# Projections with omega: the two heads of a pair alternate on the array's two halves, all of k before all of q

## The chip, the cores and the metric

The kernel runs on one core of one Trainium2 chip, with float32 throughout. A core has a matrix engine (TensorE, "PE" in the profile, with its weight loads as "PEld"), a vector engine (DVE), a scalar engine (ACT), a general engine (POOL) and a queue engine (SP), each with an instruction stream of its own; they wait for one another by semaphores. Matrix products land in PSUM, from which DVE and ACT fetch them. The metric is the device time of one execution in microseconds; lower is better.

## What is computed

Two blocks follow each other. The first is attention by random features for 8 batches of 8 heads, 576 rows, 64 columns; the second mixes its output by a Fourier transform over rows and columns, normalises it and sends it through two channel products (512 to 2048 to 512).

```python
def phi(x):                                   # q and k, scaled by 64 ** -0.25
    proj = np.einsum('bhsd,md->bhsm', x, omega)        # omega: 128 x 64
    h = proj - np.sum(x * x, axis=-1, keepdims=True) / 2.0
    h = h - np.max(h, axis=-1, keepdims=True)
    return np.exp(h) / np.sqrt(m)
q_p, k_p = phi(q_s), phi(k_s)
kv = np.einsum('bhsm,bhsd->bhmd', k_p, v); z = np.sum(k_p, axis=2)
out = einsum('bhsm,bhmd->bhsd', q_p, kv) / (einsum('bhsm,bhm->bhs', q_p, z) + 1e-6)
...
mixed = np.real(np.fft.fft(np.fft.fft(x, axis=1), axis=2))
u = x + mixed
un = (u - mean(u)) / np.sqrt(var(u) + 1e-06)
result = u + np.maximum(un @ w_ch1, 0.0) @ w_ch2
```

The change touches only the products `proj` of k and of q with omega.

## The kernel before, in words

**Attention.** `attn(b)` walks over the four pairs of heads of a batch. For a pair it transposes k (`tps` from `kn`, line 194) into `kT` and q (`tps` from `qn`) into `qT`; both have 128 partitions, head 0 of the pair on partitions 0 to 63 and head 1 on 64 to 127. `omT` holds omega transposed, once on each half. A product with omega contracts over 64 partitions, so it uses one half of the array's rows: `kT[rows, r, :]` is loaded as weights (64 by 96) and `omT[rows, :]` streams past it (128 columns). There are six such products for k (`kp`, line 245) and six for q (`qp`, line 254) for each head. A float32 matmul stands in the trace as two passes, each with a weight load, so six products are 12 passes. `features` then fetches the result on DVE (row maximum `kemx`/`qemx`, line 204; subtraction to `ke`/`qe`, line 206) and takes the exponential on ACT (line 212). Behind it follow `kvp` (269) from `ke` and v, the transposes `eps` (280) of `qe`, their copy `qeT` (286), and `ndp` (295), which gives the output rows.

**Mixing and channel products.** `mix(b)` does the Fourier products `yp` (326) and `ab` (343), the normalisation (`un`, 371), its transposes `tp` (382) and the reversal `fp` (396). `mlp(b)` does the two channel products `hp` (411) and `op` (430), with the fetches `ht` (420 on DVE, 422 on ACT) and `ot` (440), and the transposes `otp` (446).

**Weights.** The two channel weights come as 64-bit numbers; `weights()` turns them into float32 in 64 pieces: a DMA to `raw` (148), seven operations on DVE (153 to 167), one on POOL (170).

**PSUM.** The pool `big` has two buffers of two banks each; `tps`, `kp`, `qp`, `eps` and `ab` all take turns in them. `sml` and `mmp` have two buffers of one bank each; `hp` and `op` live in `mmp`.

**What sets the order.** `weights()` runs together with `attn(0)` and `mix(0)`; then `mlp(b)` runs together with `attn(b + 1)` and `mix(b + 1)`, batch by batch, and `mlp(7)` runs alone. The generators yield at marked places and `together` interleaves them by counts. A scheduler then sorts the instructions of each engine by its own idea of when their operands are ready; the result is a fixed order for each engine. DVE, ACT and POOL work off their lists in order, and an instruction that waits holds up those behind it; what PE does with its list is read from the trace.

Of the kernel before, what the change touches and what calls it, by code (L numbers as in the profile page):

```python
# [16 lines left out]
U32 = mybir.dt.uint32  # L17
PSUM = bass.MemoryType.PSUM

# Sequence rows are kept as pairs (t, S - t), t = 0 .. S/2, in three chunks of  # L20
# 97 partitions that share their border rows: chunk c holds t = 96c .. 96c + 96.
# "lo" is the row t, "hi" the row (S - t) % S; t = 0 and t = S/2 are their own
# partners, and there lo and hi hold the same row.
NC3 = 3
CW = 96
CP = CW + 1

# The high words of the doubles 2 ** -127 and of the largest one below 2 ** 128,
# as the float32 numbers of the same bits (they keep the order of magnitudes).
HI_LOW = float(np.uint32(896 << 20).view(np.float32))  # L30
HI_HIGH = float(np.uint32((1151 << 20) - 1).view(np.float32))


def _tables(S, DM):
    """The DFT matrices in the layouts of the two contractions."""
    nk = S // 2 + 1
    t = CW * np.arange(NC3)[None, :] + np.arange(CP)[:, None]
    w = np.where((t == 0) | (t == S // 2), 0.5, 1.0)
    w[0, 1:] = 0.0
    turn = (t[:, :, None] * np.arange(nk)) % S  # L40
    ang = 2.0 * np.pi * turn / S
    cs = np.cos(ang) * w[:, :, None]
    sn = np.where(turn * 2 % S == 0, 0.0, np.sin(ang)) * w[:, :, None]
    d = 128 * np.arange(DM // 128)[None, :] + np.arange(128)[:, None]
    turn = (d[:, :, None] * np.arange(DM // 2 + 1)) % DM
    ang = 2.0 * np.pi * turn / DM
    cd = np.cos(ang)
    sd = np.where(turn * 2 % DM == 0, 0.0, np.sin(ang))
    return {
        n: np.ascontiguousarray(a).astype(np.float32)  # L50
        for n, a in dict(cs=cs, sn=sn, cd=cd, sd=sd).items()
    }
# [3 lines left out]
def kernel(  # L56
# [21 lines left out]
    R = 6  # L78
    CV = 256
    PR = S // R  # L80
    SCALE = 1.0 / math.sqrt(math.sqrt(D))
    # Both feature maps carry 1 / sqrt(MF); left out of both, it scales the term
    # that is added to the denominator.
    DEN_EPS = 1e-6 * MF
    assert MF == 128 and D == 64 and PR == CW and NK == NC3 * CW + 1

# [12 lines left out]
    def big_tile(name):  # L99
        return big.tile([128, 2, 512], F32, name=name, tag="big")  # L100

# [1 line left out]
    loaded = {}  # L103

    def load(b, pr):
# [35 lines left out]
    w2v = moe_w_ch2.rearrange("(c p) m -> p c m", p=128)  # L141

    def narrow(dst, src):
        """float32 values of doubles (their 64-bit words), rounded: the top 20 bits of the
        mantissa are moved into place with the exponent, and the rest is added to that."""
        n = dst.shape[1]
        raw = cvt.tile([128, n, 2], U32, name="raw", tag="raw")
        nc.gpsimd.dma_start(raw[:].rearrange("p n two -> p (n two)"), src.bitcast(U32))
        lo, hi = raw[:, :, 0], raw[:, :, 1]
        ta = cvt.tile([128, n], U32, name="ta", tag="ta")  # L150
        tb = cvt.tile([128, n], U32, name="tb", tag="tb")
        # the magnitude, within the range of float32
        nc.vector.tensor_scalar(ta[:], hi, 0x7FFFFFFF, None, op0=ALU.bitwise_and)
        nc.vector.tensor_scalar(
            ta[:].bitcast(F32), ta[:].bitcast(F32), HI_LOW, HI_HIGH, op0=ALU.max, op1=ALU.min
        )
        # exponent - 1023 + 127 in eight bits
        nc.vector.tensor_scalar(
            ta[:], ta[:], 3, 0x40000000, op0=ALU.logical_shift_left, op1=ALU.bitwise_xor
        )  # L160
        nc.vector.tensor_scalar(tb[:], hi, 0x80000000, None, op0=ALU.bitwise_and)
        nc.vector.scalar_tensor_tensor(
            ta[:], ta[:], 0x7FFFFFFF, tb[:], op0=ALU.bitwise_and, op1=ALU.bitwise_or
        )
        nc.vector.tensor_scalar(tb[:], ta[:], 0xFF800000, None, op0=ALU.bitwise_and)
        rest = cvt.tile([128, n], F32, name="rest", tag="rest")
        nc.vector.scalar_tensor_tensor(
            rest[:], lo, 2.0**-52, tb[:].bitcast(F32), op0=ALU.mult, op1=ALU.mult
        )
        nc.gpsimd.tensor_tensor(out=dst, in0=ta[:].bitcast(F32), in1=rest[:], op=ALU.add)  # L170
# [8 lines left out]
                    narrow(w[:, j, f : f + CV], src[:, j, f : f + CV])  # L179
                    yield  # L180

    # omega^T, once for each head of a pair
    omT = const.tile([128, MF], F32, name="omT")
    omps = sml.tile([128, 512], F32, name="omps", tag="sml")
    nc.tensor.transpose(omps[:, 0:128], om[:].rearrange("m i d -> m (i d)"), ident[:])
# [1 line left out]

    xs = {}

# [1 line left out]
    def transposed(src):  # L191
        ps = big_tile("tps")
        for r in range(R):
# [3 lines left out]
        return ps  # L197

    def features(ps, rows, name):
        """exp(SCALE * (projection - its row's maximum)). The squared norm that the  # L200
        feature map takes off is the same over a row, so that it leaves with the maximum."""
        pr4 = ps[0:rows, :, 0:384].rearrange("p two (c m) -> p two c m", m=MF)
        mx = small.tile([rows, 2, 3], F32, name=name + "mx", tag=name + "mx")
        nc.vector.tensor_reduce(mx[:], pr4, axis=AX.X, op=ALU.max)  # L204
        e = att.tile([rows, R, MF], F32, name=name, tag=name)
        nc.vector.tensor_tensor(  # L206
            out=e[:].rearrange("p (two c) m -> p two c m", two=2),
            in0=pr4,
            in1=mx[:].unsqueeze(3).to_broadcast([rows, 2, 3, MF]),
            op=ALU.subtract,  # L210
        )
        nc.scalar.activation(out=e[:], in_=e[:], func=AF.Exp, scale=SCALE)  # L212
        return e

    def attn(b):
        x = xs[b] = xp.tile([CP, R, DM], F32, name="x", tag="x")
        for pr in range(NP):
# [6 lines left out]
                func=AF.Copy,  # L224
            )
            yield
            # q in the order of the pairs: lo t = 0 .. 288, hi t = 0 .. 288
            qps = transposed(qn)
            qT = att.tile([128, 2 * NK], F32, name="qT", tag="qT")
            qsrc = qps[:, :, 0:288].rearrange("q two (c p) -> q two c p", p=CW)  # L230
# [6 lines left out]
            for at, p in ((NK - 1, CW // 2), (NK, 0)):  # L237
                nc.vector.tensor_copy(out=qT[:, at : at + 1], in_=qps[:, 0, p : p + 1])  # L238
            yield
            kes, qes = [], []  # L240
            for i in range(2):
                rows = slice(D * i, D * i + D)
                kp = big_tile("kp")
                for r in range(R):
                    nc.tensor.matmul(  # L245
                        kp[0:PR, r // 3, r % 3 * MF : r % 3 * MF + MF],
                        lhsT=kT[rows, r, :],
                        rhs=omT[rows, :],
                    )
                kes.append(features(kp, PR, "ke"))  # L250
                qp = big_tile("qp")
                for r in range(R):
                    t0 = r // 3 * NK + r % 3 * CW
                    nc.tensor.matmul(  # L254
                        qp[0:CP, r // 3, r % 3 * MF : r % 3 * MF + MF],
                        lhsT=qT[rows, t0 : t0 + CP],
                        rhs=omT[rows, :],
                    )
                qes.append(features(qp, CP, "qe"))
                yield  # L260
            # the next pair's loads run ahead
            n = b * NP + pr + 2
            if n < B * NP:
                load(n // NP, n % NP)
# [39 lines left out]
                )  # L304
                yield

# [1 line left out]
    uns = {}  # L308

    def mix(b):  # L310
        x = xs[b]
        # over the sequence, folded on the pairs: rows 0 .. S/2 are enough
        y = fft.tile([128, 2, NDC, NK], F32, name="y", tag="y")
        for dc in range(NDC):
            cols = slice(128 * dc, 128 * dc + 128)
# [20 lines left out]
            mlpp.tile([128, NDC, NK], F32, name=f"unT{g}", tag="unT", bufs=3) for g in range(2)  # L336
        ]
        for c in range(NC3):
            # over the model: columns 0 .. DM/2 of the even and of the odd part
            ab = big_tile("ab")  # L340
            for n, tab in enumerate((cd, sd)):
                for dc in range(NDC):
# [26 lines left out]
            for g in range(2):  # L369
# [11 lines left out]
                for dc in range(NDC):  # L381
                    nc.tensor.transpose(  # L382
                        tp3[:, dc, :], un[:, 128 * dc : 128 * dc + 128], ident[0:CP, 0:CP]
                    )
                # a border row that the chunk before holds stays out; hi runs backwards,
                # into the order of the sequence
                p0 = min(c, 1)
                dst = un_t[g][:] if g == 0 else un_t[g][:, :, ::-1]
                nc.scalar.activation(
# [9 lines left out]
        for g in range(2):  # L399
            uns[b, g] = un_t[g]  # L400

# [1 line left out]
    def mlp(b):  # L403
        x = xs[b]
        for g in range(2):
# [36 lines left out]
            for c in range(NC3):  # L442
                t0 = CW * c if g == 0 else CW * (NC3 - 1 - c)
                tp = sml.tile([128, 512], F32, name="otp", tag="sml")
                for dc in range(NDC):
                    nc.tensor.transpose(  # L446
                        tp[0:CP, 128 * dc : 128 * dc + 128],
                        os_[dc][:, t0 : t0 + CP],
                        ident[:],
                    )  # L450
                u = x[:, NC3 * g + c, :]
                nc.vector.tensor_tensor(out=u, in0=u, in1=tp[0:CP, :], op=ALU.add)  # L452
                # each row once: lo gives 0 .. S/2, hi the rest
                if g == 0:
                    parts = ((0, CW), (CW, CP)) if c == NC3 - 1 else ((0, CW),)
                else:
                    parts = ((1, CW),) if c == NC3 - 1 else ((0, CW),)
                for p0, p1 in parts:
                    s0 = S // 2 * g + t0 + p0
                    nc.sync.dma_start(out[b, s0 : s0 + p1 - p0, :], u[p0:p1, :])  # L460
                yield
# [56 lines left out]
```

## Time and profile before

| what | value |
|---|---|
| three timed runs | 1859.08 to 1861.77 us, median 1860.35 us |
| the profiled execution: span from first to last instruction | 1856.5 us |
| median of the runs less that span | 3.85 us |
| busy DVE, ACT, POOL | 639.6, 358.2, 208.7 us |
| matmul passes in `kp` and `qp` | 768 and 768 |
| data moved | 57.73 MB, 31 GB/s in the mean |

The page gives no total for the profiled execution besides its span; what lies around the span is taken to be the 3.85 us by which the median of the runs exceeds it. Timeline rows below read: start, length, engine, line, operation, output and inputs, shapes, number of instructions, and in brackets the idle time before with what ended it. A row of several passes ends when its last pass has drained, so the next row may start earlier.

### The profile page before, as it was taken

The page shows a single profiled execution, that of the slowest core. Times are in us where ns is not written, and L with a number is a line of the kernel's source. Part 1 is how long each engine was busy: PE and PEld are TensorE (multiplying, and loading weights), DVE is VectorE, ACT ScalarE, POOL GpSimd, SP SyncE. Part 2 cuts the span into 40 slices and gives each one's busy share as a digit, 9 for nine tenths or more (in the row PEclk, how much of TensorE's full clock was granted, in tenths as well). Part 3 has the DMA queues.
Part 4 walks back from the last instruction along what each step waited for, and adds up shares of the span by engine and source line. Part 5 has one row for each costly group of instructions (what it writes and reads, how often), then busy time and mean ns, then how long its engine had stood idle before and what let it go on. Part 6 is the DMA issues. An engine that isn't in the chain of part 4 may idle for free.

```text
span 1856.5 us, 21861 instructions
## 1 busy us (share of the span) xinstructions
PE 1752.1 (94%) x9137; PEld 1409.8 (76%) x9137; DVE 639.6 (34%) x1450; ACT 358.2 (19%) x641; POOL 208.7 (11%) x319
## 2 busy tenths in 40 slices
PE   5997988999999899999999999998999999998998
PEld 5885766877888688877888678886888778886776
DVE  5777873313242323313233132413233132332000
ACT  1221121112121212212221121212122121211100
POOL 2335331010001200011001100012000110012000
PEclk9997978999999999999999999999999999999999
DMA  6322322001110101101010011101011010000000
GB/s 145 82 79 71 93 76 55 7 1 26 26 45 7 26 20 29 24 7 26 20 40 20 9 24 23 43 7 26 20 33 26 1 26 20 20 1 13 1 13 13
DMA packets 125013, 57.73 MB, mean 31 GB/s; under 512 B 115762, under 2 KB 115762, under 8 KB 124916
## 3 DMA queue, kind: packets, MB, share of 16 engines
q1 hardware_dynamic: 119248, 37.83, 8.7%
q0 software_dynamic: 5120, 16.78, 2.8%
q10 hardware_dynamic: 548, 1.73, 0.4%
q8 instruction: 73, 1.20, 0.3%
q14 instruction: 24, 0.20, 0.0%
HBM read 46.88 MB, written 9.44 MB: 30 GB/s over the span
## 4 chain that ended last, share of the span: by engine, by line
PE 82%; DVE 7%; POOL 4%; DMA 4%; issue 2%; ACT 1%; POOLq 0%; SPq 0%; DVEq 0%; ACTq 0%
PE hp L411 26%; PE op L430 24%; PE yp L326 5%; PE kvp L269 5%; PE kp L245 4%; PE qp L254 4%; PE ndp L295 4%; PE ab L343 4%; DMA raw<-in_moe_w_ch_dram 4%; PE eps L280 2%; POOL x L359 1%; PE fp L396 1%; PE tp L382 1%; PE tps L194 1%; PE otp L446 1%
## 5 line engine op out<-in xcount | busy, mean ns | idle before, releaser
L430 PE MATMUL op<-ht,w 128*128 128x289 f32 x2048 | 531.7, 413 | 8.2 <-POOL w L170 8.2
L411 PE MATMUL hp<-unT,w 128*128 128x289 f32 x2048 | 532.5, 414 | 0.0
L430 PEld LDWEIGHTS op<-ht,w 128*128 128x128 f32 x2048 | 387.5, 192 | 116.9 <-POOL w L170 9.5
L411 PEld LDWEIGHTS hp<-unT,w 128*128 128x128 f32 x2048 | 387.0, 193 | 114.7 <-issue 8.7
L420 DVE TENSOR_SCALAR ht<-hp 128x289 f32<-128x289 f32 x128 | 58.8, 459 | 374.6 <-PE hp L411 374.6
L254 PE MATMUL qp<-omT,qT 64*97 64x128 f32 x768 | 112.1, 299 | 15.8 <-DVE qT L238 14.6
L245 PE MATMUL kp<-omT,kT 64*96 64x128 f32 x768 | 114.5, 302 | 5.3 <-DVE ke L206 2.9
L254 PEld LDWEIGHTS qp<-omT,qT 64*97 64x97 f32 x768 | 100.5, 182 | 22.8 <-issue 15.9
L245 PEld LDWEIGHTS kp<-omT,kT 64*96 64x96 f32 x768 | 98.5, 180 | 25.4 <-issue 17.9
L422 ACT ACTIVATE ht<-hp 128x289 f32<-128x289 f32 x128 | 52.8, 412 | 296.7 <-PE hp L411 296.7
L269 PEld LDWEIGHTS kvp<-v,ke 96*128 96x128 f32 x768 | 103.5, 209 | 6.9 <-issue 1.1
L269 PE MATMUL kvp<-v,ke 96*128 96x65 f32 x768 | 105.3, 291 | 0.0
L212 ACT ACTIVATE ke<-ke 96x768 f32<-96x768 f32 x64 | 53.8, 841 | 213.5 <-DVE ke L206 213.5
L295 PEld LDWEIGHTS ndp<-kv,qeT 128*97 128x97 f32 x768 | 82.3, 180 | 10.3 <-ACT qeT L286 2.0
L353 DVE TENSOR_TENSOR bmp<-ab,bmp 97x257 f32<-97x257 f32 x24 | 10.2, 423 | 221.4 <-ACT bmp L352 221.4
L204 DVE TENSOR_REDUCE kemx<-kp 96x6 f32<-96x768 f32 x64 | 60.8, 950 | 70.4 <-PE kp L245 70.4
L295 PE MATMUL ndp<-kv,qeT 128*97 128x65 f32 x768 | 82.6, 262 | 1.6 <-DVE kv L277 1.3
L452 DVE TENSOR_TENSOR x<-x,otp 97x512 f32<-97x512 f32 x48 | 32.5, 683 | 148.6 <-PE otp L446 148.6
L113 POOL MEMSET v<- 96x12 f32 x32 | 3.7, 116 | 700.6 <-PE kvp L269 694.0
L286 ACT ACTIVATE qeT<-eps 128x582 f32<-128x582 f32 x64 | 42.0, 656 | 192.9 <-PE eps L280 174.2
L321 POOL TENSOR_TENSOR fold<-x 97x384 f32<-97x384 f32 x32 | 40.1, 1252 | 331.7 <-PE kvp L269 242.2
L440 ACT ACTIVATE ot<-op 128x289 f32<-128x289 f32 x64 | 26.4, 412 | 255.4 <-PE op L430 255.4
(65 smaller groups left out, 1558.8 us busy)
## 6 DMA issues: line engine op xcount, KB each, us to landing
raw<-in_moe_w_ch_dram POOLq DMA_DIRECT2D x64, 256.0 KB, 3.0
kn<-in_k_dram SPq DMA_DIRECT2D x64, 144.0 KB
qn<-in_q_dram SPq DMA_DIRECT2D x64, 144.0 KB
v<-in_v_dram SPq DMA_DIRECT2D x64, 144.0 KB
out_dram<-x SPq DMA_DIRECT2D x40, 192.0 KB
out_dram<-x SPq DMA_DIRECT2D x8, 190.0 KB
cd_sb<-k_cd ACTq DMA_DIRECT2D x1, 385.5 KB
sd_sb<-k_sd ACTq DMA_DIRECT2D x1, 385.5 KB
```

The costliest lines, as they stand in the source:

```text
L204: nc.vector.tensor_reduce(mx[:], pr4, axis=AX.X, op=ALU.max)
L212: nc.scalar.activation(out=e[:], in_=e[:], func=AF.Exp, scale=SCALE)
L245: nc.tensor.matmul(kp[0:PR, r // 3, r % 3 * MF : r % 3 * MF + MF], lhsT=kT[rows, r, :], rhs=omT[rows, :],)
L254: nc.tensor.matmul(qp[0:CP, r // 3, r % 3 * MF : r % 3 * MF + MF], lhsT=qT[rows, t0 : t0 + CP], rhs=omT[rows, :],)
L269: nc.tensor.matmul(kvp[:, 0 : D + 1], lhsT=kes[i][:, r, :], rhs=v1[:, i, r, :], start=(r == 0), stop=(r == R - 1),)
L295: nc.tensor.matmul(nd[:, r, :], lhsT=qeT[:, r, :], rhs=kv[:])
L326: nc.tensor.matmul(yp[:, 0:NK], lhsT=f[:, c, :], rhs=tab[:, c, :], start=(c == 0), stop=(c == NC3 - 1),)
L343: nc.tensor.matmul(ab[0:CP, n, 0:KD], lhsT=y[:, n, dc, CW * c : CW * c + CP], rhs=tab[:, dc, :], start=(dc == 0), stop=(dc == NDC - 1),)
L411: nc.tensor.matmul(hp[:, 0:NK], lhsT=w1[:, dc, 128 * fc : 128 * fc + 128], rhs=un_t[:, dc, :], start=(dc == 0), stop=(dc == NDC - 1),)
L420: nc.vector.tensor_scalar(ht[:], hp[:, 0:NK], 0.0, None, op0=ALU.max)
L422: nc.scalar.activation(out=ht[:], in_=hp[:, 0:NK], func=AF.Relu)
L430: nc.tensor.matmul(op_[:, 0:NK], lhsT=w2[:, fc, 128 * dc : 128 * dc + 128], rhs=hs[fc][:], start=(fc == 0), stop=(fc == NFC - 1),)
```

## The change

The loop over the two heads moves inside. First come the 12 products of k, head 0 and head 1 in turn, into two tiles of `big`; then `features` of both; then a yield; then the same for q. The number of products, fetches and exponentials stays the same, and so do all shapes. Line numbers behind it fall by five.

```diff
             kes, qes = [], []
-            for i in range(2):
-                rows = slice(D * i, D * i + D)
-                kp = big_tile("kp")
+            for name, rows_out, made in (("k", PR, kes), ("q", CP, qes)):
+                ps = [big_tile(name + "p") for _ in range(2)]
                 for r in range(R):
-                    nc.tensor.matmul(
-                        kp[0:PR, r // 3, r % 3 * MF : r % 3 * MF + MF],
-                        lhsT=kT[rows, r, :],
-                        rhs=omT[rows, :],
-                    )
-                kes.append(features(kp, PR, "ke"))
-                qp = big_tile("qp")
-                for r in range(R):
-                    t0 = r // 3 * NK + r % 3 * CW
-                    nc.tensor.matmul(
-                        qp[0:CP, r // 3, r % 3 * MF : r % 3 * MF + MF],
-                        lhsT=qT[rows, t0 : t0 + CP],
-                        rhs=omT[rows, :],
-                    )
-                qes.append(features(qp, CP, "qe"))
+                    for i in range(2):
+                        rows = slice(D * i, D * i + D)
+                        t0 = r // 3 * NK + r % 3 * CW
+                        nc.tensor.matmul(
+                            ps[i][0:rows_out, r // 3, r % 3 * MF : r % 3 * MF + MF],
+                            lhsT=kT[rows, r, :] if name == "k" else qT[rows, t0 : t0 + CP],
+                            rhs=omT[rows, :],
+                        )
+                made += [features(ps[i], rows_out, name + "e") for i in range(2)]
                 yield
```

The rest of the diff removes comments.

What the scheduler makes of it on PE, in the second pair of a batch in the steady part (the pair that stands at 696 us in the trace of before), before the change:

```order
L245 MATMUL kp<-omT,kT 96x128 x6
L254 MATMUL qp<-omT,qT 97x128 x6
L430 MATMUL op<-ht,w_133 128x289 x8
L245 MATMUL kp<-omT,kT 96x128 x6
L254 MATMUL qp<-omT,qT 97x128 x6
L269 MATMUL kvp<-v_4811,ke 128x65 x6
L430 MATMUL op<-ht,w_133 128x289
L280 MATMUL eps<-ident,qe 128x97 x6
L430 MATMUL op<-ht,w_133 128x289 x7
L295 MATMUL ndp<-kv,qeT 97x65 x6
```

The same place on PE with the change:

```order
L249 MATMUL kp<-omT,kT 96x128 x12
L425 MATMUL op<-ht,w_133 128x289 x8
L249 MATMUL qp<-omT,qT 97x128 x12
L264 MATMUL kvp<-v_4811,ke 128x65 x6
L425 MATMUL op<-ht,w_133 128x289 x6
L275 MATMUL eps<-ident,qe 128x97 x6
L425 MATMUL op<-ht,w_133 128x289 x2
L290 MATMUL ndp<-kv,qeT 97x65 x6
```

Where a head's k and q stood next to each other, both heads' k now stand together, and both heads' q; the eight `op` between stay; five of the `op` move from behind the first `eps` to ahead of it. In this pair the twelve products alternate head by head, in each of the two blocks.

In the third pair the scheduler doesn't keep the alternation. PE with the change, with the tiles' numbers (`kp_4525`, `qp_4549` are head 0; `kp_4526`, `qp_4550` head 1):

```order
L249 MATMUL kp_4525<-omT_134,kT_4494 96x128 x5
L249 MATMUL kp_4526<-omT_134,kT_4494 96x128 x5
L249 MATMUL kp_4525<-omT_134,kT_4494 96x128
L249 MATMUL kp_4526<-omT_134,kT_4494 96x128
L441 MATMUL otp_4573<-ident_111,ot_4346 97x128
```

Before, the same place reads:

```order
L245 MATMUL kp_4525<-omT_134,kT_4494 96x128 x6
L254 MATMUL qp_4537<-omT_134,qT_4511 97x128 x6
L446 MATMUL otp_4573<-ident_111,ot_4346 97x128
L446 MATMUL otp_4573<-ident_111,ot_4428 97x128
L446 MATMUL otp_4573<-ident_111,ot_4476 97x128
```

Five products of one head come in a row, then five of the other. Over the whole program, 425 of the 768 products stand directly behind one of the other tile of projections with the change (56 before).

On DVE in the second pair, with the change (`kemx_4336`, `ke_4338` belong to head 0, `kemx_4341`, `ke_4343` to head 1):

```order
L204 TENSOR_REDUCE kemx_4336<-kp_4322 96x6
L204 TENSOR_REDUCE kemx_4341<-kp_4323 96x6
L206 TENSOR_TENSOR ke_4338<-kp_4322,kemx_4336 96x768
L206 TENSOR_TENSOR ke_4343<-kp_4323,kemx_4341 96x768
L204 TENSOR_REDUCE qemx_4371<-qp_4357 97x6
```

And before:

```order
L204 TENSOR_REDUCE kemx_4329<-kp_4322 96x6
L206 TENSOR_TENSOR ke_4331<-kp_4322,kemx_4329 96x768
L204 TENSOR_REDUCE qemx_4341<-qp_4334 97x6
L206 TENSOR_TENSOR qe_4343<-qp_4334,qemx_4341 97x768
L204 TENSOR_REDUCE kemx_4364<-kp_4357 96x6
```

Both maxima now stand ahead of both subtractions, so the first buffer of `big` is given back by the third operation where it was the second.

At the very start of the program, DVE with the change takes the next piece of weights ahead of the first head's maximum:

```order
L238 COPY qT_194<-tps_187 128x1 x2
L153 TENSOR_SCALAR ta_201<-raw_199 128x256
L161 TENSOR_SCALAR tb_202<-raw_199 128x256
L154 TENSOR_SCALAR ta_201<-ta_201 128x256
L204 TENSOR_REDUCE kemx_239<-kp_225 96x6
L158 TENSOR_SCALAR ta_201<-ta_201 128x256
L153 TENSOR_SCALAR ta_214<-raw_212 128x256
```

Before, the maximum and the subtraction of that head stood ahead of it:

```order
L238 COPY qT_194<-tps_187 128x1 x2
L204 TENSOR_REDUCE kemx_232<-kp_225 96x6
L206 TENSOR_TENSOR ke_234<-kp_225,kemx_232 96x768
L153 TENSOR_SCALAR ta_201<-raw_199 128x256
L161 TENSOR_SCALAR tb_202<-raw_199 128x256
```

So there the fetch of `kp_225` moves behind the arrival of the piece `raw_199`.

## The prediction

> **What bounds the kernel now.** I read the page first, then the stretches of equal length.
>
> ```profile
> PE 1752.1 (94%) x9137; PEld 1409.8 (76%) x9137; DVE 639.6 (34%) x1450; ACT 358.2 (19%) x641; POOL 208.7 (11%) x319
> PE 82%; DVE 7%; POOL 4%; DMA 4%; issue 2%; ACT 1%; POOLq 0%; SPq 0%; DVEq 0%; ACTq 0%
> 641.00:856.00 215.00, 209.77 (x1144) 168.72 (x1143) 63.31 (x126) 44.59 (x80) 14.92 (x23) 0.98 0.09 23
> 1071.00:1286.00 215.00, 209.69 (x1144) 168.60 (x1143) 63.29 (x126) 44.58 (x80) 14.63 (x23) 0.98 0.09 23
> 292.81 7.44 PE L430 MATMUL op<-ht,w 128*128 128x289 f32 x21 [4.19 <-POOL w L170]
> ```
>
> PE is busy 94% and holds 82% of the chain that ended last. A batch in the steady part takes 215 us, PE busy 209.7 of it and DVE 63, and one batch looks like the next: there, time saved on PE is time saved, if no wait takes its place. The last row shows the other regime: until 293 us PE waits for weights. So three stretches: weights to about 293 us, six whole batches beside `mlp(1)` to `mlp(6)`, and `mlp(7)`, which has no projections.
>
> **What a block of projections costs.** The second pair of a batch and, from the third, a block of one half alone:
>
> ```profile
> 696.31 1.55 PE L245 MATMUL kp<-omT,kT 64*96 64x128 f32 x12
> 697.70 1.47 PE L254 MATMUL qp<-omT,qT 64*97 64x128 f32 x12
> 699.10 4.16 PE L430 MATMUL op<-ht,w 128*128 128x289 f32 x16
> 703.19 1.55 PE L245 MATMUL kp<-omT,kT 64*96 64x128 f32 x12
> ...
> 711.85 1.17 PE L295 MATMUL ndp<-kv,qeT 128*97 128x65 f32 x12
> 712.85 4.11 PE L430 MATMUL op<-ht,w 128*128 128x289 f32 x16
> ...
> 736.79 1.55 PE L245 MATMUL kp<-omT,kT 64*96 64x128 f32 x12
> 738.27 1.55 PE L269 MATMUL kvp<-v,ke 96*128 96x65 f32 x12
> ```
>
> From the first `kp` to the `op` behind `qp` it takes 699.10 - 696.31 = 2.79 us for 24 passes, all on one half of the rows. Twelve passes alone, with the way into and out of the half-height shape, take 738.27 - 736.79 = 1.48 us. So if both halves run at once, a block of 24 passes costs 1.48 us and the lag of the second half behind the first.
>
> **Do the halves run at once?** Before, head 0's `kp` and `qp` share a half, and head 1's block mostly comes later, so it can be seen at one place only, in the first pair, at half clock (a pass each 0.21 us, where 1.39/12 = 0.11 to 0.12 us is the steady part's):
>
> ```profile
> 25.26 0.39 PEld L245 LDWEIGHTS kp<-omT,kT 64*96 64x96 f32 x2
> 25.29 0.49 PE L245 MATMUL kp<-omT,kT 64*96 64x128 f32 x1
> 25.44 0.41 PE L254 MATMUL qp<-omT,qT 64*97 64x128 f32 x1
> 25.44 0.28 PEld L254 LDWEIGHTS qp<-omT,qT 64*97 64x97 f32 x1
> 25.58 0.42 PE L245 MATMUL kp<-omT,kT 64*96 64x128 f32 x1
> 25.58 0.28 PEld L245 LDWEIGHTS kp<-omT,kT 64*96 64x96 f32 x1
> 25.65 0.41 PE L254 MATMUL qp<-omT,qT 64*97 64x128 f32 x1
> 25.66 0.28 PEld L254 LDWEIGHTS qp<-omT,qT 64*97 64x97 f32 x1
> 25.79 0.42 PE L245 MATMUL kp<-omT,kT 64*96 64x128 f32 x1
> 25.79 1.99 PEld L245 LDWEIGHTS kp<-omT,kT 64*96 64x96 f32 x9
> 25.87 0.41 PE L254 MATMUL qp<-omT,qT 64*97 64x128 f32 x1
> 26.00 2.12 PE L245 MATMUL kp<-omT,kT 64*96 64x128 f32 x9
> ```
>
> These `kp` are head 1's, these `qp` head 0's. Head 0's passes start at 25.44, 25.65, 25.87, head 1's at 25.58, 25.79, 26.00: each half keeps its 0.21 us, so two halves do twice the work. Head 1's first pass also starts ahead of three of head 0's that stand before it in the program, so the halves need not alternate in the list: it is enough that both are in PE's queue. The weight loads overlap too: four start within 0.35 us (25.44 to 25.79). Head 0's pass ahead of 25.44 is due at 25.23, and head 1 joins at 25.29: a lag of 0.06 us at half clock; I take 0.04.
>
> A whole block then costs 1.48 + 0.04 = 1.52 us where it cost 2.79: **1.27 us saved**, the lag being the only part of it that is chosen. Bounds: nothing, if the halves take turns at full clock, and 2.79 - 1.48 = 1.31.
>
> Against this stands the Trainium skill, "TensorE: Matmul & The Clock Gate", Part 3: four row tiles measured 3.07 times one, not four. An estimate by that share of 0.77 makes a block about 0.4 us dearer and the forecast about 13 us later; the rows above show no such loss, but over three passes only.
>
> **Waits in place of the old ones.** Both q products need both buffers of `big` back, so DVE must fetch both k's.
>
> ```profile
> 697.90 0.95 DVE L204 TENSOR_REDUCE kemx<-kp 96x6 f32<-96x768 f32 x1 [3.96 <-PE kp L245]
> 698.89 0.95 DVE L206 TENSOR_TENSOR ke<-kp,kemx 96x768 f32<-96x768 f32 x1
> 699.76 0.94 DVE L204 TENSOR_REDUCE qemx<-qp 97x6 f32<-97x768 f32 x1
> 700.74 0.96 DVE L206 TENSOR_TENSOR qe<-qp,qemx 97x768 f32<-97x768 f32 x1
> ...
> L212 ACT ACTIVATE ke<-ke 96x768 f32<-96x768 f32 x64 | 53.8, 841 | 213.5 <-DVE ke L206 213.5
> L286 ACT ACTIVATE qeT<-eps 128x582 f32<-128x582 f32 x64 | 42.0, 656 | 192.9 <-PE eps L280 174.2
> ```
>
> DVE starts 1.59 us after the first `kp` (697.90 - 696.31) and takes 3.80 us for the four (to 701.70). With the overlap both k's are done at about the time that one was, so the second buffer is free 1.63 + 3.80 = 5.43 us after the block's start. PE comes back to q after 1.52 us and the eight `op`, 703.19 - 699.10 = 4.09: at 5.61. Covered, by 0.2 us, in the second pair and likewise in the fourth (`hp` there). If the cover went, each block would wait by what DVE is late; one more operation like these ahead would be 0.95 - 0.2, about 0.75 us a block. Behind q, `eps` needs DVE's first three operations and an exponential, 0.3 + 2.9 + 0.84 = 4.0 us from the last pass; ahead of it stand `kvp` (12 passes, some 1.4) and six `op` (6/8 of 4.09 = 3.1): covered. In the third pair `ndp` follows `eps` by one `hp` (4.09/8 = 0.5 us) and four short transposes, some 0.8 us, while the copy `qeT` takes 0.66 us and a wait on either side: even, and I count 0.1 us.
>
> **Where nothing is saved.** The first pair:
>
> ```profile
> 853.07 1.55 PE L245 MATMUL kp<-omT,kT 64*96 64x128 f32 x12
> 855.65 1.75 PE L254 MATMUL qp<-omT,qT 64*97 64x128 f32 x12 [1.03 <-DVE qT L238]
> 857.86 1.55 PE L382 MATMUL tp<-ident,un 97*128 97x97 f32 x8 [0.45 <-DVE un L371]
> ```
>
> `qp` waits 1.03 us for the copies that end in `qT`. Head 1's `kp`, which now stands there, needs the buffer from which these copies read, so it starts at the same time, and `tp` waits for `un` either way: 0. In the third pair the k block is the same case (five products, then five), saving about 0.2 us.
>
> **A steady batch.** Five whole blocks (first pair's q, both of the second and fourth pair): 5 x 1.27 = 6.35. Third pair: 0.2 for k; its head-1 products stood apart, two times 1.48, now one block: 2.96 - 1.52 = 1.44; less 0.1: 1.5 in all. Together 7.9 us of 215. Six batches: **47 us**. Beside `mlp(0)` only one block comes after 293 us: 1.3.
>
> **The start.** Until 293 us the weights set the end, so nothing saved on PE counts by itself. But the first pair loses:
>
> ```profile
> 24.19 0.95 DVE L206 TENSOR_TENSOR ke<-kp,kemx 96x768 f32<-96x768 f32 x1
> 26.32 0.29 DVE L153 TENSOR_SCALAR ta<-raw 128x256 uint32<-128x256 uint32 x1 [1.18 <-DMA raw<-in_moe_w_ch_dram]
> 31.42 0.92 PE L254 MATMUL qp<-omT,qT 64*97 64x128 f32 x3 [0.54 <-DVE qe L206]
> ```
>
> Head 0's fetch, done at 25.14, now stands behind operations that wait for a piece of weights until 26.32; with thirteen short ones (at most 0.29 each), two maxima and two subtractions (0.95 each) up to the end of head 1's fetch, its buffer is free at about 26.3 + 3.5 + 3.8 = 33.6 us, and `qp` of head 1 starts there, not at 31.42: about 2 us later, and what stands behind it in DVE's list with it. In pairs 2 to 4 head 1's k takes the slot of head 0's q, and nothing changes. I take +2; bounds -3 (weights come earlier, since DVE waits less for PE) and +6 (the delay is paid again in each chain of that pair).
>
> Sum: 47 + 1.3 - 2 = 46 us off the profiled span of 1856.5 gives 1810; with the 3.85 by which the median of the runs exceeds that span, **1814 us**.
>
> **The clock.** Once a batch it falls to half:
>
> ```profile
> 638.35:641.75 3.40, 2.37 (x22) 2.19 (x21) 2.48 (x8) 1.04 (x2) 1.40 (x3) 1.00 0.81 195
> 641.77:648.58 6.81, 6.37 (x19) 4.00 (x18) 3.59 (x5) 3.04 (x5) 0.45 (x1) 0.50 0.08 17
> 842.00:845.40 3.40, 1.74 (x8) 1.02 (x6) 2.32 (x7) 0.41 (x1) 1.49 (x3) 1.00 0.00 0
> ```
>
> For 6.8 us after the thin stretch with the first pair's projections, costing about 3.4 us; the still thinner stretch at 842 us (1.74 of 3.40 busy) brings none, so place counts too. A shorter batch shifts that place: from no dip (-20 us in six batches) to a second one (+20).
>
> **Rivals.**
> 1. Only neighbours in the list overlap, because passes start in program order. The third pair's q (four, then four) loses most of its gain, about 0.9 us, and alternating blocks cost one pass (0.11 us) more: 0.9 + 5 x 0.11 = 1.4 a batch, 9 us in six: 1823. Against it: three passes were overtaken at 25.3 us. The Trainium skill, "TensorE: Matmul & The Clock Gate", Part 3, states such an order of starts; by that overtaking the trace disagrees. This is also the case that the change does not do what it says, since 273 products stand behind one of their own tile.
> 2. Matmuls overlap, weight loads queue. An `ndp` pass, set by its load of 97 columns, takes (712.85 - 711.85)/12 = 0.083 us; a block is then 1.48 with its 12 passes (0.11 each) replaced by 24 loads, 1.48 - 1.32 + 1.99 = 2.15, saving 0.64, half of the forecast: 24 us less, 1838. Against it: the loads above.
> 3. A second dip a batch: 1814 + 20 = 1834.
> 4. The halves take turns at full clock: no saving, and the start's 2 us: 1862, within 0.2%.
> 5. Slower: as 4, but DVE's list at the start delays the whole chain of the first pair (k's fetch, q's fetch, exponential, `eps`) and the weights with it, +6: 1866. It decides once overlap brings less than 1 us a batch. For it: DVE waits for the piece of weights at 26.32. Against it: the overlap seen.
>
> **Chances.** Forecast 0.70, own range 1804 to 1824; rival 1 0.10; 2 0.07; 3 0.05; 4 0.04; 5 0.04. Faster 0.92, the same 0.04, slower 0.04, by 0.2%, which is about what a measurement can tell. The range 1802 to 1836 holds the forecast's bounds (start, waits, some change of dips), rival 1 and 3.
>
> **What would show it.** Right: a `kp` row of 24 passes whose block takes about 1.5 us, `kp` and `qp` at about half their busy time, batches of 207 to 208 us, no idle time of PE ahead of `qp` in pairs 2 and 4. Wrong: blocks of 2.2 or 2.8 us, PE waiting for `ke` by more than a few tenths, a second half-clock stretch in a batch, or weights done well after 296 us.

## The result and the profile after

| | before | changed |
|---|---|---|
| median of four runs each | 1860.96 us | 1818.88 us |
| lowest to highest | 1859.08 to 1861.77 | 1817.86 to 1819.99 |
| span of the profiled execution | 1856.5 us | 1818.1 us |

The ratio is 0.978, with a 95% interval of 0.976 to 0.979: 42 us less, where the forecast was 46. The profiled execution of the changed kernel took 1819.99 us, 1.9 us more than its span.

The page of the changed kernel, with busy time of the engines, the chain's shares, and the groups of the two products:

```profile
PE 1713.1 (94%) x9137; PEld 1366.9 (75%) x9137; DVE 633.9 (35%) x1450; ACT 357.3 (20%) x641; POOL 207.7 (11%) x319
PE 82%; DVE 7%; POOL 4%; DMA 4%; issue 2%; ACT 1%; POOLq 0%; SPq 0%; DVEq 0%; ACTq 0%
L249 PE MATMUL kp<-omT,kT 64*96 64x128 f32 x768 | 98.3, 313 | 19.7 <-DVE qT L238 18.9
L249 PE MATMUL qp<-omT,qT 64*97 64x128 f32 x768 | 74.4, 299 | 5.2 <-DVE ke L206 5.1
```

PE is busy 39 us less, and its share stays at 94%: the time that the products gave up was not filled with waits. Before, the same two groups read:

```profile
L245 PE MATMUL kp<-omT,kT 64*96 64x128 f32 x768 | 114.5, 302 | 5.3 <-DVE ke L206 2.9 <-DVE qT L238 1.6 <-DVE bmp L354 0.6
L254 PE MATMUL qp<-omT,qT 64*97 64x128 f32 x768 | 112.1, 299 | 15.8 <-DVE qT L238 14.6 <-DVE qe L206 1.2
```

Their busy time fell to 86% and 66%, where the prediction had named "about half" as a sign of being right. Two batches in the steady part, in the view by stretches (length, busy time of PE, PE's weight loads, DVE, ACT and POOL, then granted clock):

```profile
849.00:1056.85 207.85, 202.35 (x1144) 161.24 (x1143) 62.14 (x125) 44.51 (x80) 14.91 (x23) 0.98 0.10 24
1056.85:1264.72 207.87, 202.39 (x1143) 161.19 (x1142) 62.14 (x125) 44.52 (x80) 14.63 (x23) 0.98 0.10 23
```

A batch takes 207.9 us where it took 215.0. The second pair of a batch in the timeline of PE, and DVE's rows at the same place:

```profile
689.75 1.55 PE L249 MATMUL kp<-omT,kT 64*96 64x128 f32 x24
691.23 4.16 PE L425 MATMUL op<-ht,w 128*128 128x289 f32 x16
695.32 1.55 PE L249 MATMUL qp<-omT,qT 64*97 64x128 f32 x24
696.81 1.55 PE L264 MATMUL kvp<-v,ke 96*128 96x65 f32 x12
```

```profile
691.33 1.82 DVE L204 TENSOR_REDUCE kemx<-kp 96x6 f32<-96x768 f32 x2 [3.96 <-PE kp L249]
693.07 1.81 DVE L206 TENSOR_TENSOR ke<-kp,kemx 96x768 f32<-96x768 f32 x2
```

From `kp` to the `op` behind it are 691.23 - 689.75 = 1.48 us for 24 passes, and 1.49 for `qp`; it was 2.79. DVE gives the second buffer back at 693.07 + 1.81 = 694.88, and `qp` starts at 695.32 with no idle time ahead of it.

The third pair, whose k the scheduler had put into the list as five products of head 0, five of head 1, then one each, and whose q as four, four, then in turn:

```profile
723.78 2.78 PE L249 MATMUL kp<-omT,kT 64*96 64x128 f32 x24
726.50 0.68 PE L441 MATMUL otp<-ident,ot 128*97 128x128 f32 x4
...
729.55 2.07 PE L249 MATMUL qp<-omT,qT 64*97 64x128 f32 x24
731.55 1.55 PE L264 MATMUL kvp<-v,ke 96*128 96x65 f32 x12
```

There k takes 726.50 - 723.78 = 2.72 us and q 731.55 - 729.55 = 2.00. In both blocks head 1 had to wait for the second buffer of `big`, which DVE gives back:

```profile
724.68 0.22 DVE L238 COPY qT<-tps 128x1 f32<-128x1 f32 x2
728.14 1.81 DVE L206 TENSOR_TENSOR ke<-kp,kemx 96x768 f32<-96x768 f32 x2
```

The copies end at 724.90, and in PE's instructions head 1's first k pass starts at 725.05, behind the ten passes of head 0's five products. The second `ke` ends at 729.95, 0.40 us after the q block began, and head 1's first q pass starts at 730.10, with three of head 0's eight passes still to come. So these two blocks do not tell what the order in the list costs; a later experiment does. And the first pair:

```profile
632.24 1.55 PE L249 MATMUL kp<-omT,kT 64*96 64x128 f32 x12
634.82 1.52 PE L249 MATMUL kp<-omT,kT 64*96 64x128 f32 x12 [1.03 <-DVE qT L238]
637.03 1.36 PE L377 MATMUL tp<-ident,un 97*128 97x97 f32 x8 [0.69 <-DVE un L366]
```

The same wait of 1.03 us for `qT` that stood ahead of `qp` stands ahead of head 1's `kp` now, and from the first product to `tp` it is 4.79 us in both kernels.

Where the 38.4 us between the two spans arose, by the same product in both traces: the first `hp` of `mlp(0)` comes 3.2 us later than before and the first of `mlp(1)` 1.0 us later; then the six batches from `mlp(1)` to `mlp(6)` win 7.0, 6.1, 7.2, 7.2, 6.2 and 7.1 us, 40.7 together; what comes behind them loses 1.4.

### The profile page after: what moved, and what is told of

Read it like the earlier page. It is cut to its first block, busy times and chain, and to the rows that moved or that the text cites. A ratio compares the mean times of both kernels' runs of the same rounds, so it can differ in the third digit from the quotient of the medians.

```text
span 1818.1 us, 21866 instructions
## 1 busy us (share of the span) xinstructions
PE 1713.1 (94%) x9137; PEld 1366.9 (75%) x9137; DVE 633.9 (35%) x1450; ACT 357.3 (20%) x641; POOL 207.7 (11%) x319
## 4 chain that ended last, share of the span: by engine, by line
PE 82%; DVE 7%; POOL 4%; DMA 4%; issue 2%; ACT 1%; POOLq 0%; SPq 0%; DVEq 0%; ACTq 0%
PE hp L406 27%; PE op L425 24%; PE yp L321 5%; PE kvp L264 5%; PE ab L338 4%; PE ndp L290 4%; DMA raw<-in_moe_w_ch_dram 3%; PE kp L249 3%; PE qp L249 3%; PE eps L275 2%; PE fp L391 2%; POOL x L354 1%; PE tps L194 1%; PE tp L377 1%; DVE st L358 1%
## 5 line engine op out<-in xcount | busy, mean ns | idle before, releaser
L406 PEld LDWEIGHTS hp<-unT,w 128*128 128x128 f32 x2048 | 391.0, 195 | 119.0 <-issue 8.7
L249 PE MATMUL kp<-omT,kT 64*96 64x128 f32 x768 | 98.3, 313 | 19.7 <-DVE qT L238 18.9
L249 PEld LDWEIGHTS kp<-omT,kT 64*96 64x96 f32 x768 | 85.0, 187 | 34.5 <-issue 24.2
L249 PE MATMUL qp<-omT,qT 64*97 64x128 f32 x768 | 74.4, 299 | 5.2 <-DVE ke L206 5.1
L249 PEld LDWEIGHTS qp<-omT,qT 64*97 64x97 f32 x768 | 65.4, 179 | 18.1 <-issue 14.6
L170 POOL TENSOR_TENSOR w<-ta,rest 128x256 f32<-128x256 f32 x64 | 52.7, 823 | 172.3 <-DVE rest L167 169.6
```

The costliest lines, as they stand in the source:

```text
L249: nc.tensor.matmul(ps[i][0:rows_out, r // 3, r % 3 * MF : r % 3 * MF + MF], lhsT=kT[rows, r, :] if name == "k" else qT[rows, t0 : t0 + CP] ...
L406: nc.tensor.matmul(hp[:, 0:NK], lhsT=w1[:, dc, 128 * fc : 128 * fc + 128], rhs=un_t[:, dc, :], start=(dc == 0), stop=(dc == NDC - 1),)
```

## The experiments

### Do the halves work at once, or is it the grouping?

Theory A: two halves of the rows work at once. Theory B: the new grouping saves, by fewer switches and other waits. In `same_half` every instruction keeps its place in every list, and only the rows change:

```diff
-                        rows = slice(D * i, D * i + D)
+                        rows = slice(0, D)
```

> The instructions of every engine stay in the order of the changed kernel, but head 1's products read head 0's half of kT, qT and omT (rows 0 to 63), so head 1's features are made from head 0's rows; the output differs from the reference there. Theory A (the gain is that two halves of the rows work at once): a steady block of 24 alternating passes goes from 1.49 us back to about 2.79, the third pair's q block from 2.00 to about 2.8; per batch 5 x 1.30 + 0.8 = 7.3 us, six batches 44, with the one block beside mlp(0) 1.3: 1818.9 + 45 = 1864 us (1859 to 1869), at or just above the kernel before. Theory B (the gain is the new grouping: fewer switches, other waits of PE for DVE): blocks keep what they cost by grouping, time stays at 1819 us (1816 to 1823).

Measured: 1863.64 us, ratio to before 1.0025 (1.0016 to 1.0034). The view by stretches and the second pair's k block in the timeline:

```profile
865.10:1080.10 215.00, 209.72 (x1144) 168.57 (x1143) 62.14 (x125) 44.42 (x80) 14.94 (x23) 0.98 0.09 23
```

```profile
700.13 2.86 PE L249 MATMUL kp<-omT,kT 64*96 64x128 f32 x24
702.91 1.97 PE L425 MATMUL op<-ht,w 128*128 128x289 f32 x7
```

The block takes 702.91 - 700.13 = 2.78 us and the batch 215.0 again. The time is some 4 to 5 us above before, and 3.8 of it stand in the trace already at the first `hp` of `mlp(1)`, where the changed order loses. With the order alone nothing is won; Theory B is out.

### How near must the halves stand in the list?

`no_alt` turns the two loops round, so that six products of head 0 stand ahead of six of head 1:

```diff
-                for r in range(R):
-                    for i in range(2):
+                for i in range(2):
+                    for r in range(R):
```

`run2` and `run3` alternate in runs of two and three products. An edge from each product to the one before it, which orders the list and waits for nothing, keeps the scheduler to it:

```diff
+                done = None
+                for i, r in [(i, r + j) for r in range(0, R, 2) for i in range(2) for j in range(2)]:
...
-                        nc.tensor.matmul(
+                    ins = nc.tensor.matmul(
...
+                    if done is not None:
+                        tc.add_manual_dep(ins.ins, done.name, IN_ORDER, reason="order")
+                    done = ins.ins
```

> The changed kernel with the loops turned round: in each block six products of head 0, then six of head 1, each on its own half; the result is the same. Theory A (halves overlap only while the passes stand within about 2 or 3 of one another in PE's list): head 1's first pass starts when 2 or 3 of head 0's 12 are still to start, a steady block takes 2.36 to 2.47 us, 0.9 to 1.0 more than 1.49; the third pair's q stands as two blocks of six (2.96 for 2.00); per batch 5 x 0.95 + 0.96 = 5.7, six batches 34, 1 beside mlp(0): 1854 us (1848 to 1859). Theory C (the order in the list doesn't matter, both in PE's queue is enough, as the prediction said): blocks of 1.5 us, only the third pair's q dearer by 0.96: 1825 us (1820 to 1828). Theory B (grouping alone): 1819 to 1825.

> The changed kernel with the heads alternating in runs of two products (four passes of head 0, four of head 1, and so on), held in that order by edges between the products that cost no wait; the result is the same. With a look-ahead of 2 passes a steady block takes 1.59 us, with 3 or more 1.48, with none (starts strictly in the list's order) 2.25. Theory A (look-ahead of 2 to 3): 1.48 to 1.59, per batch at most 5 x 0.1 more and some tenths less in the third pair, where q now stays in runs: 1819 to 1822 us. Strict order of starts: 5 x 0.76 = 3.8 a batch, 1842 us.

> The same with runs of three products (six passes). A steady block takes 2.47 us with starts strictly in order, 1.81 with a look-ahead of 2 passes, 1.70 with 3, 1.59 with 4, 1.48 with 5 or more. Theory A (2 to 3): 1.70 to 1.81, per batch 5 x 0.2 to 0.33 more, less about 0.2 to 0.3 in the third pair's q: 1825 us (1821 to 1830). Theory C (order doesn't matter): 1.48, 1816 to 1819 us.

Measured: `no_alt` 1858.47 us (ratio 0.9996, 0.9987 to 1.0006), `run2` 1812.86 (0.975, 0.9735 to 0.9764), `run3` 1831.36 (0.9844, 0.9828 to 0.9861). The second pair's k block in each, in the order `no_alt`, `run2`, `run3`:

```profile
693.60 2.50 PE L249 MATMUL kp<-omT,kT 64*96 64x128 f32 x24
696.04 1.73 PE L425 MATMUL op<-ht,w 128*128 128x289 f32 x6
```

```profile
679.16 1.63 PE L252 MATMUL kp<-omT,kT 64*96 64x128 f32 x24
680.72 1.49 PE L431 MATMUL op<-ht,w 128*128 128x289 f32 x5
```

```profile
688.16 1.85 PE L252 MATMUL kp<-omT,kT 64*96 64x128 f32 x24
689.94 1.73 PE L431 MATMUL op<-ht,w 128*128 128x289 f32 x6
```

| run of one head in the list | products 1 | 2 | 3 | 6 |
|---|---|---|---|---|
| block of 24 passes, measured | 1.48 us | 1.56 | 1.78 | 2.44 |
| head 1's first pass starts behind head 0's first by | 0.01 us | 0.01 | 0.30 | 0.96 |
| passes of head 0's first run still to start then | 1 | 3 | 3 | 3 |
| 1.48 plus that delay | 1.49 | 1.49 | 1.78 | 2.44 |

The second and third rows are read from the single passes in the traces. These are the passes that had started just ahead of head 1's first one, in `no_alt`, `run3` and `run2`:

```profile
693.60 1.22 PE L249 MATMUL kp<-omT,kT 64*96 64x128 f32 x9
688.16 0.56 PE L252 MATMUL kp<-omT,kT 64*96 64x128 f32 x3
679.16 0.35 PE L252 MATMUL kp<-omT,kT 64*96 64x128 f32 x1
```

Nine of 12, three of six, one of four: each time three passes that stand before it were still to come. So a pass may overtake three passes that wait for the other half, and the delay that is left makes the block longer. The expectations had left two or three open; for three they gave 1.48, 1.70 and 2.36 us, 0.08 too little each time. With runs of 3 and 6 that is because they took 0.109 us from the first pass of a half to its second, which the traces show as 0.19. With runs of 2, where head 1 starts almost at once, 0.07 us are lost in one later pass (0.18 us to the next, at 679.68); why is open. A product is two passes, and of the four spacings alternating single products is the only one that costs nothing.

The times have a second part. `run3` loses 3.6 us a batch against the changed kernel (5 x 0.30 = 1.5 in its blocks, and up to 1.7 by a second half-clock stretch, shown below) and `run2` 0.6, yet `run2` is 5 to 6 us faster than the changed kernel: its last piece of weights is done at 283.2 us, that of `run3` at 285.5, that of the changed kernel at 297.8. In the first batch the changed kernel's list holds mostly six of one head, then six of the other; the edges spread them. The expectation, which counted steady batches only, missed this, and the next runs ask about it. `no_alt` is 4 us above its expectation: besides the 5.7 us of its blocks, its batches have a second half-clock stretch.

```profile
827.66:831.07 3.41, 3.41 (x8) 1.85 (x7) 0.00 (x0) 0.92 (x2) 0.00 (x0) 0.51 0.00 0
855.06:861.89 6.83, 6.49 (x17) 4.27 (x18) 3.30 (x5) 3.05 (x5) 0.00 (x0) 0.50 0.02 5
```

The first of these, with PE busy throughout, costs 3.41/2 = 1.7 us in a batch; 5.7 + 1.7 = 7.4, against 6.7 measured in the mean of the six batches and 7.3 where the other stretch is as long in both kernels.

### The start: what the weights wait for

Four kernels change the order in some places only. `first_old` has before's order in the first batch alone. The other three use the edges: `start_alt` alternates single products in the first batch, `steady_q3` in the third pair of batches 2 to 8, `run1` everywhere.

```diff
+            if b == 0:
+                for i in range(2):
...
+            else:
+                for name, rows_out, made in (("k", PR, kes), ("q", CP, qes)):
```

```diff
-                    if done is not None:
+                    if done is not None and b == 0:
```

The first diff is that of `first_old`, the second that of `start_alt`; in `steady_q3` the condition reads `b > 0 and pr == 2`, in `run1` it is left out.

> The changed kernel, but the first batch's attention (beside which the weights come) in the order of before: head 0's k and q, then head 1's; the result is the same. From the second batch on the order is that of the changed kernel. The changed kernel reaches the first hp 3.3 us later than before, the 128th op 2.4 later. Theory S (the loss at the start comes from the first batch's new order, as the prediction said): 1818.9 - 2.4 = 1816.5 us (1815 to 1818). Rival (it comes from somewhere else, or from half-clock stretches that lie differently by chance): 1819 (1817 to 1821).

> The changed kernel with edges that keep head 0 and head 1 in turn within each block of products, in the first batch's attention alone (the changed kernel there has six of one head, then six of the other); later batches have the changed kernel's order. Theory P (the prediction's step: until the weights are there nothing saved on PE counts): 1819 us (1816 to 1822), last piece of weights done at 298 us as now. Theory Q (PE's products, DVE's fetches behind them and DVE's conversion of weights hang on one another in that stretch, so PE's time there counts): as with runs of two and three (last piece at 283 and 286 us), last piece at 282 to 286 us, 1806 us (1803 to 1810).

> The changed kernel with the same edges in the third pair of batches 2 to 8 alone, whose k and q the changed kernel's list holds as five and five, and four and four. In the list k now stands as one product, then eleven in turn, q likewise. By the split blocks of the run with runs of two (0.60 us for a piece of two products, so 0.39 for one; 1.49 for the rest) k takes 1.87 instead of 2.71, q 1.87 instead of 2.00. Theory A (PE's time counts there, DVE keeps up): 0.97 a batch, six batches 5.8: 1813 us (1811 to 1816). Rival (PE then waits for DVE's fetches or for the exponential instead): 1819 (1816 to 1820).

> The changed kernel with the edges in every block of products of every batch. Theory Q and A together: the start gains 12.5 us as in the run with runs of two, the third pair 1.0 a batch, the first pair's k, now split in three pieces around tp and hp, loses about 0.7 a batch: 1818.9 - 12.5 - 6 x 0.3 = 1804.6 us (1801 to 1808). Theory P with A: 1817 us. If the three single gains add up, this run is start_alt plus steady_q3 less what the first pair's split costs.

Measured: `first_old` 1820.31 us (ratio 0.9789, 0.9775 to 0.9802), `start_alt` 1806.22 (ratio 0.9713, 0.97 to 0.9726), `steady_q3` 1815.63 (0.9751, 0.973 to 0.9773), `run1` 1811.86 (0.9737, 0.9724 to 0.9751).

- `first_old`: Theory S falls. The first `hp` comes 4.2 us earlier than in the changed kernel, about where it stood before, but the last piece of weights comes at 301.3 us, and the end is no earlier.
- `start_alt`: Theory P falls. The last piece comes at 280.6 us, 17 us earlier, and the run is about 12.5 us faster than the changed kernel (12.7 by the medians, 12.1 by the ratios to before), as Theory Q expected.
- `steady_q3`: the blocks became what was expected, in the timeline of the third pair:

```profile
721.82 0.46 PE L252 MATMUL kp<-omT,kT 64*96 64x128 f32 x2
722.20 0.68 PE L447 MATMUL otp<-ident,ot 128*97 128x128 f32 x4
722.72 0.65 PE L412 MATMUL hp<-unT,w 128*128 128x289 f32 x2
723.30 1.55 PE L252 MATMUL kp<-omT,kT 64*96 64x128 f32 x22
724.78 3.19 PE L412 MATMUL hp<-unT,w 128*128 128x289 f32 x12
```

k takes 0.38 + 1.48 = 1.86 us. Yet its five runs lie between 1809.0 and 1819.8, wider than those of any other kernel here. In the profiled one (1817.8) the six batches together are 0.4 us shorter instead of 5.9, and the half-clock stretches in them add up to 60.3 us against 50.5 in the changed kernel: 9.8 us more at half clock are up to 4.9 us lost, enough to take back most of the gain. What lengthens these stretches stays open.
- `run1` missed its expectation by 7 us. Of the 12.5 us by which `start_alt` reaches the first `hp` of `mlp(1)` sooner, 8.3 are there, and the six batches together are 0.4 us longer than in the changed kernel, where 1.8 less was expected; most of them have a half-clock stretch of 10.2 us. The gains don't add, and what takes them back is not shown.

`start_alt` is faster either because PE's products are shorter (Theory Q), or because the edges moved DVE's list so that more pieces of weights stand ahead of the same step of attention (Theory R). `start_half` keeps every list of `start_alt` and takes the overlap away, in the first batch alone:

```diff
-                    rows = slice(D * i, D * i + D)
+                    rows = slice(D * i, D * i + D) if b else slice(0, D)
```

> The kernel with the edges in the first batch (start_alt), instruction for instruction in the same order on every engine, but in the first batch head 1's products read head 0's half of kT, qT and omT, so its features are made from head 0's rows and the output differs there; two halves never work at once in that batch. Theory Q (PE's time counts while the weights come): the gain of start_alt goes, last piece of weights at 296 to 299 us, 1819 us (1816 to 1822). Theory R (DVE sets the pace there, and start_alt is faster because its list on DVE has more pieces of weights ahead of the same step of attention: 25 against 20 ahead of the fourth pair's maxima, 149 against 162 other operations ahead of the last piece): last piece at 280 to 284 us, 1807 us (1804 to 1810).

Measured: 1815.86 us (0.977, 0.9757 to 0.9783), last piece at 290.2 us; so the overlap, Theory Q, holds 9.6 us of the gain by the medians (10.6 by the ratios), and the lists, Theory R, 3.0 (1.5), which the intervals don't separate from nothing. Neither expectation was met; the run lies nearer to Theory Q's. What PE's time does there is seen in DVE's waits up to the last piece, `start_alt` first, then `start_half` (what DVE waited for, us in total, times, longest):

```profile
DVE qemx L207 <- PE qp L252: 1.3, 2, 0.7
```

```profile
DVE qemx L207 <- PE qp L252: 7.3, 4, 2.8
...
DVE kemx L207 <- PE kp L252: 3.9, 4, 2.1
```

Without the overlap DVE waits 7.3 + 3.9 - 1.3 = 9.9 us more for the products, and the last piece comes 290.2 - 280.6 = 9.6 us later. DVE converts the weights and fetches the products from one list; when it waits for a product, the pieces behind it wait too. The ends of the last piece of weights, in the changed kernel, `start_alt` and `start_half`:

```profile
297.10 0.72 POOL L170 TENSOR_TENSOR w<-ta,rest 128x256 f32<-128x256 f32 x1 [2.01 <-DVE rest L167]
279.89 0.73 POOL L173 TENSOR_TENSOR w<-ta,rest 128x256 f32<-128x256 f32 x1 [3.29 <-DVE rest L170]
289.52 0.73 POOL L173 TENSOR_TENSOR w<-ta,rest 128x256 f32<-128x256 f32 x1 [3.29 <-DVE rest L170]
```

The first `hp` comes later in `start_half` too, at 208.2 us instead of 197.5: the overlap moves the first batch as a whole, and the run does not separate its attention from its weights.

### Both places together

> The edges in the first batch and in the third pair of the later ones, nowhere else; the result is the same. If the two gains add: 1818.9 - 12.7 (start_alt) - 3.3 (steady_q3) = 1803 us (1799 to 1806); by the third pair's blocks in the trace of steady_q3 (0.386 + 1.478 us for k instead of 2.71, 0.386 + 1.479 for q instead of 2.00: 0.98 a batch, 5.9 in six) and without any other change 1800. Rival (half-clock stretches take back what the third pair saves, as 10.2 us instead of 6.8 in a batch do with 1.7 us each): 1806 us.

Measured: 1803.93 us (0.9716, 0.9703 to 0.9729; 1800.3 to 1808.9). It beats the changed kernel by 15 us by the medians and by 11.5 by the ratios (0.9778 - 0.9716 = 0.0062 of 1859), but can't be told from `start_alt` by their intervals. So what is shown is the gain of the start, some 0.6%; that of the third pair is seen in its blocks and not in the medians. In the profiled execution, the fastest of the five, the six batches together are 4.2 us shorter than in the changed kernel, where 5.9 was expected.

## Why the prediction was right, and where it was not

- **The block, 1.27 us saved.** Right, and a little small: 2.79 - 1.48 = 1.31, since the second half lags by 0.007 us between starts instead of 0.04. `same_half` shows that the overlap is all of it. Rival 2 (weight loads queue, 2.15 us) and rival 4 (halves take turns) are out. By an estimate from the Trainium skill's 3.07 times for four row tiles ("TensorE: Matmul & The Clock Gate", Part 3), a block would have taken 1.9 us; for two halves no run here shows such a loss.
- **"The halves need not alternate in the list: it is enough that both are in PE's queue."** This step failed. At 25.3 us three passes were overtaken, and the prediction stretched three into any number; there head 1 came in when its buffer did (DVE's fetch ends at 25.14), so the rows could not show a limit. The runs of 2, 3 and 6 products show it: three passes, and six products in a row cost 0.95 us a block. The changed kernel paid little for this step in its steady batches, since pairs 2 and 4 alternate.
- **The third pair.** Its q was mis-sized: the prediction gave it 1.52 us, as if both buffers were free, and it took 2.00, with the second buffer 0.40 us late. It saved 2.96 - 2.00 = 0.96 instead of 1.44. For k the prediction named the wait for the buffer rightly, but 0.08 was saved instead of 0.2. Rival 1 expected 0.9 us of loss in q, where 0.48 came, for another reason, and an extra pass in alternating blocks, of which there is none.
- **Waits.** Right: in the second pair the second buffer is free 0.44 us ahead of `qp`, where 0.2 was expected, and PE shows no idle time there. The first pair's k block gained nothing, as expected. In the view of groups between 300 and 1700 us all of `qp` has no idle time ahead of it, and the 6.2 us of `kp` are the first pairs' wait for `qT`, once a batch:

```profile
L249 PE MATMUL kp<-omT,kT 64*96 64x128 f32 x588 | 57.9, 282 | 6.2 <-DVE qT L238 6.2
L249 PE MATMUL qp<-omT,qT 64*97 64x128 f32 x600 | 42.0, 276 | 0.0
```

- **A steady batch, 7.9 us.** Measured 7.1, and 6.1 in two of the six. Five blocks give 5 x 1.30 = 6.5 and the third pair 1.0, which is 0.4 too much. The half-clock stretch, as long as before, now lies over more of PE's work (6.8 us of 6.8, where the prediction's row at 641.77 has 6.4); that this takes the 0.4 is argued, not shown. In the two batches of 6.1 us it is longer:

```profile
637.34:644.16 6.82, 6.82 (x18) 4.25 (x17) 2.68 (x4) 3.04 (x5) 0.00 (x0) 0.50 0.00 0
842.11:852.35 10.24, 9.46 (x29) 6.87 (x30) 5.22 (x12) 3.04 (x5) 0.70 (x1) 0.50 0.23 53
```

  Six batches: 40.7 instead of 47. Of the 6.3 us of difference 2.9 are the third pair's q and 0.7 its k, the blocks gave 0.9 back, and the rest, some 4, is put down to the clock without a run that isolates it. Rival 3, a second stretch, did not come in this kernel; it did in `no_alt` and `run3`.
- **The start, -2 us and mlp(0) +1.3.** The sum came out by luck (the first `hp` of `mlp(1)` stands 1.0 us later); the reasons didn't. The loss at the first `hp` is there, 3.2 us, and before's order takes it away, but the end does not follow. "Until 293 us the weights set the end, so nothing saved on PE counts by itself" failed: PE's products hold up DVE, and DVE holds up the weights and the rest of the first batch, by some 10 us. The changed kernel wins nothing there, since its list hardly alternates in that batch.
- **What lies around the span, 3.85 us.** Mis-sized. The executions whose time and span are both known lie 1.9 us apart (1819.99 and 1818.1). So the profiled execution of before, with 1856.5 + 1.9 = 1858.4, was one of its faster ones. The 2 us too many brought the forecast of 1814 nearer to the 1818.9 measured, by luck: the span was forecast at 1810 and is 1818.1.

## What to carry to other kernels

Products that use half the rows should alternate half by half, one product each, in the engine's final list: read that list, since a scheduler that sorts by readiness takes the alternation out just where a buffer comes free late, and an edge that costs no wait puts it back. Where the second buffer is late, put other work between the first product and the rest, as `steady_q3` has it: its k took 1.86 us of PE instead of 2.72. An engine off the bound can be on the path through another engine's list: before calling time in a stretch worthless, look what the bounding engine waits for there, and add it up. When a gain shows in the blocks and not in the total, look at the clock before the waits.

## What was not expected of the hardware

- **A short look-ahead.** In the blocks of `no_alt`, `run2` and `run3` shown above, a pass on the free half starts ahead of three passes that wait for the other half, not more. In the changed kernel's alternating block at 689.75 us the two passes of each step start 6 to 8 ns apart.
- **Half-clock stretches come in steps.** In the steady part they last 3.41, 6.83 or 10.24 us, one, two or three times 3.41. The Trainium skill, "TensorE: Matmul & The Clock Gate", Part 1, states that the window over which the clock is set is free-running and 3413 ns long. The rows agree. One in which PE is busy throughout runs at half clock too (the row at 827.66 above); why a batch gets one, two or three such steps no run here settles.
- **The granted clock of the first stretch is not always on record.** Up to 125 us, passes of the products on one half start 0.213 us apart in every trace here, twice the 0.109 of the steady part. Yet the view by stretches gives a clock of 0.50 for `start_alt` and 1.00 for `both`, which have the same lists there and the same busy times:

```profile
80.00:150.00 70.00, 48.90 (x258) 42.21 (x258) 51.75 (x151) 13.30 (x20) 24.03 (x38) 0.50 0.32 89
```

```profile
80.00:150.00 70.00, 49.00 (x257) 42.21 (x257) 51.93 (x151) 13.20 (x19) 24.15 (x38) 1.00 0.31 90
```

  The first record of the clock stands at 67 us in the trace of `start_alt` and at 152 us in that of `both`; ahead of it the column reads 1.00, and there the spacing of equal passes is the better clock. At half clock PE's products cost double, which may be one reason why they counted in the start.
